# A spectral mixing and SwiGLU kernel: the last step of the inverse transform as four products of 96 columns

## The chip, the cores and the metric

The kernel runs on one core of a Trainium2 chip. The metric is the device time of one execution in microseconds (us). A core has five engines that run side by side: TensorE (PE; its weight loads are listed as PEld), VectorE (DVE), ScalarE (ACT), GpSimd (POOL) and SyncE (SP, which here only issues DMA transfers). Each engine takes its instructions in the order of the program and waits for others at semaphores. Everything is computed in fp32.

## The reference

Two blocks stand one behind the other. The first filters each of 8 sequences (3008 tokens, 256 channels) in the frequency domain. The second is a feed-forward block with a SwiGLU.

```python
X = np.fft.rfft(x, axis=1)                      # x: 8 x 3008 x 256
y = np.fft.irfft(X * (filt_r + 1j*filt_i), n=3008, axis=1)
t = y.reshape(24064, 256)
g, val = t @ w_gate, t @ w_val                  # 256 x 1536 each
out = (g / (1 + np.exp(-g)) * val) @ w_out      # 1536 x 256
```

## The kernel before

The length 3008 is 47 x 64, and so a transform is done in two steps each way, with twiddle factors in the tables. A token has the number n1 * 64 + n2, with n1 from 0 to 46 and n2 from 0 to 63. The step that is changed is the last one of the inverse transform, `stage3`: for each n2 it adds up 24 coefficients s (real and imaginary part) with a table of cosines and sines to the 47 values of n1. The signal is real, so 24 of the 47 coefficients are enough.

A batch is worked on in 4 chunks k. Each chunk has two halves i, each half two blocks cb of 128 channels; `step` counts these four sub-steps. In batch 0 a sub-step has four products of 96 rows (2 halves x 48) and 94 columns. From batch 1 on it has three products, packed so that all 128 rows are used:

```python
BACK = (((0, 0, 0, 48), (1, 48, 0, 48), (2, 96, 0, 32)),
        ((4, 64, 0, 48), (5, 112, 0, 16), (2, 0, 32, 16), (3, 16, 0, 48)),
        ((5, 0, 16, 32), (6, 32, 0, 48), (7, 80, 0, 48)))
BACK_AT = (0, 3 * N1, 7 * N1)                   # N1 = 47

# class Spectral: the coefficients of a half chunk come from DRAM
def load_t4(self, k, i, part=None):             # the branch for b > 0
    t = t4pool.tile([128, NH, C], FP32, ...)    # NH = 4, C = 256; 2 buffers
    rows = self.d2_tokens.rearrange("(h n) a c -> h (n a) c", h=2)
    rows = rows[:, ts(at, 2 * NS * NH)]         # NS = 24
    for j in range(2):
        self.load(out=t[64*j:64*j+64, 1], in_=rows[j, 128*(1-j):128*(1-j)+64])
        self.load(out=t[:, 2*j], in_=rows[j, 64*j:64*j+128])

def stage3(self, k, step):
    i, cb = divmod(step, 2)
    ps = (self.bank if k == 0 else fbank)(...)  # fbank too for k == 0 when b > 0
    for j in range(len(BACK) if back else 0):   # back = b: from batch 1 on
        cols = back_t[0][:, first:first + N1 * len(BACK[j])]     # 141, 188, 141
        pin(nc.tensor.matmul(out=rows, lhsT=self.t4[k, i][:, j, ts(cb, 128)], rhs=cols, ...))
    # batch 0: four products [96 rows] x [94 columns of wi_t]
    yield
    if cb == 0:
        pin(nc.scalar.copy(out=tokens(2 * i, 2), in_=psv))       # 376 elements
        return
    for t in range(2):                          # KS = (-1, 0, 1, 2)
        a, c = 2 * i + t, psv[:, :, ts(t, N1)]
        b, v, k = tokens(a, 1), tokens(4 + a, 1), KS[a]
        # k == 0: scalar.copy(v, c);  k == -1: vector add(v, c, b)
        # else:   vector v = c - k * b                           # 188 elements
```

The result `y` of a chunk has the tokens side by side, so that a sub-step writes every fourth element (16 bytes apart). All spectral steps of the batches from 1 on share one PSUM bank:

```python
fps = pool("fps", 1, PSUM)                      # one buffer
wps = pool("wps", NB, PSUM)                     # NB = 7, for the feed-forward products
def fbank(name):
    return fps.tile([128, NV, C], FP32, name=name, tag="f")
```

The feed-forward block runs at the same time, on the batch before. It works in groups, and the order of its operations is written out as a list of tokens. P, Q, A, B, E and W are products; s, x, y, e, l, h, v, o are operations that are mostly VectorE's; f, c, m, g, u are ScalarE's; D, S, n are GpSimd's. The tokens t0.0, t0.1 and so on are the slots in which spectral work is slipped in: up to five pieces a group (the first digit), and each slot carries a piece on to its next `yield`.

```python
SCHEDULE = """
Q0 o3' t4.2' W2 f0 S00' S01' x0.o' t0.0 x1.o' Q1 t0.1 x2.o' P3 x3.o' f1 t4.3' W1 x4.o' S10' x03 S11'
s13 x5.o' P1 o1 t0.2 P0 o2 c1 D01 A13 g1 c0 S20' Q2 S21' g0 y01 m13 t1.0 h0 f2 s01 W6 t1.1 h1 x23
D02 P2 o6 D12 A01 c2 B13 g2 n3' m01 t0.3 S30' t1.2 x02 W7 S31' g13 y12 y02 B01 h13 o7 t1.3 t2.0 s02
... # (cut)
E23 t3.2 m03 v13 E01 l23 e03 t3.3 t4.0 l01 u23 B23 v23 u01 t4.1 E03 n1 v01 g23 B03 l03 W3 h23 g03
u03 h03 v03
""".split()
```

The token h of a feed-forward group, for instance, is one VectorE product of 188 elements from PSUM with an SBUF operand (line L907). Products of the groups have 188 columns (L860) or 128 columns (L939).

Of the kernel before, what the change touches and what calls it, by code (L numbers as in the profile page):

```python
# [53 lines left out]
N1, N2 = 47, 64  # L54
# [58 lines left out]
PIECES = ((0, 7), (7, 14), (14, 20), (20, 26))  # L113

BACK = (((0, 0, 0, 48), (1, 48, 0, 48), (2, 96, 0, 32)),
        ((4, 64, 0, 48), (5, 112, 0, 16), (2, 0, 32, 16), (3, 16, 0, 48)),  # L120
        ((5, 0, 16, 32), (6, 32, 0, 48), (7, 80, 0, 48)))
BACK_AT = (0, 3 * N1, 7 * N1)


def dft_tables():
    n1, n2 = np.arange(N1), np.arange(N2)
    s, q = np.arange(NS), np.arange(NQ)
    ph = 2 * np.pi * (np.outer(n1, s) % N1) / N1
    w = np.stack([np.cos(ph), -np.sin(ph)], 1)
    wf = np.zeros((N1, 2, NS, 2, 2))  # L130
    wi = np.zeros((NS, 2, 2, N1, 2))

    v = np.stack([2 * np.cos(ph), -2 * np.sin(ph)], 0)
    v[0, :, 0], v[1, :, 0] = 1.0, 0.0
    for h in range(2):
        wf[:, h, :, :, h] = w.transpose(0, 2, 1)
        wi[:, :, h, :, h] = v.transpose(2, 0, 1) / S
    one = wi[:, :, 0, :, 0].transpose(1, 0, 2).reshape(2 * NS, N1)
    back = np.zeros((128, 10 * N1))
    for tile_, first in zip(BACK, BACK_AT):  # L140
        for i, (_, row, a, rows) in enumerate(tile_):
            back[row:row + rows, first + N1 * i:first + N1 * (i + 1)] = one[a:a + rows]


    kap = np.where(q[:, None] < 32, s + N1 * q[:, None], s + N1 * (95 - q[:, None]))
    sg = np.where(q < 32, 1.0, -1.0)[:, None]
    th = 2 * np.pi * ((n2[:, None, None] * kap) % S) / S
    c, sn = np.cos(th), np.sin(th)
    d = np.zeros((2, N2, NS, 2, NQ))
    d[0, :, :, 0] = c.transpose(0, 2, 1)  # L150
    d[1, :, :, 0] = sn.transpose(0, 2, 1)
    d[0, :, :, 1] = (-sn * sg).transpose(0, 2, 1)
    d[1, :, :, 1] = (c * sg).transpose(0, 2, 1)
    d = d.reshape(128, NS, 128)
    de = np.stack([d, d.transpose(2, 1, 0)], 2)

    paired = np.zeros((NP * (NPAIR + 1), 2, NP, NS))
    for j in range(NP):
        paired[NPAIR * j:NPAIR * (j + 1), :, j] = w[1:NPAIR + 1]
        paired[NP * NPAIR + j, 0, j] = 1.0  # L160
    paired = paired.reshape(NP * (NPAIR + 1), -1)


    pairs = np.arange(128).reshape(2, N2).T.ravel()
    later = np.stack([de[:, :, 0], de[:, :, 1][:, :, pairs]], 2)
    f32 = np.float32
    return (wf.reshape(NR, NK).astype(f32), wi.reshape(NK, NR).astype(f32),
            back.astype(f32), paired.astype(f32), np.ascontiguousarray(de).astype(f32),
            np.ascontiguousarray(later).astype(f32))


@with_exitstack
def kernel(
# [8 lines left out]
    out: bass.AP,  # L182
):
    nc = tc.nc
    wf_host, wi_host, back_host, paired_host, de_host, later_host = dft_tables()
    wf_dram = nc.inline_tensor(wf_host, name="wf_tbl")
    wi_dram = nc.inline_tensor(wi_host, name="wi_tbl")
    paired_dram = nc.inline_tensor(paired_host, name="paired_tbl")
    back_dram = nc.inline_tensor(back_host, name="back_tbl")
    de_dram = nc.inline_tensor(de_host, name="de_tbl").ap()  # L190
    later_dram = nc.inline_tensor(later_host, name="later_tbl").ap()
    unit_dram = nc.inline_tensor(np.eye(128, dtype=np.float32), name="unit_tbl")

    def pool(name, bufs, space=None):
# [63 lines left out]
    def sub(eng, dst, a, b):  # L258
        return eng.tensor_tensor(out=dst, in0=a, in1=b, op=ALU.subtract)  # L259
# [226 lines left out]
    def load_back():  # L486

        for n in range(3):
            t = rpool.tile([128, 2, 128], U32, name=f"paired_{n}", tag="pw", bufs=3)
            t = t.bitcast(FP32).rearrange("p b f -> p (b f)")  # L490
            (differences if n else paired_t).append(t[0:NP * (NPAIR + (not n))])
        t = rpool.tile([128, 2, 128, 2], U32, name="x_third", tag="raw", bufs=2)
        t = t.bitcast(FP32).rearrange("p b f two -> p (b f two)")
        third.append(t[0:NP * (NPAIR + 1)].rearrange("p (i c) -> p i c", c=C))
        pin(nc.sync.dma_start(out=paired_t[0][:, 0:2 * NP * NS], in_=paired_dram.ap()))
        t = rpool.tile([128, 2, 128, 2], U32, name="back", tag="raw", bufs=2)
        t = t.bitcast(FP32).rearrange("p b f two -> p (b f two)")
        back_t.append(t[:, 0:10 * N1])
        pin(nc.sync.dma_start(out=back_t[0], in_=back_dram.ap()))


# [13 lines left out]
    class Spectral:  # L515


        def __init__(self, b):
            self.b = b
            self.d1, self.d2 = [dram_tiles[2 * (b % 2) + i] for i in range(2)]  # L520
            self.d1_rows = self.d1.rearrange("a (h n) c -> (a h) n c", h=2)

            self.d2_tokens = self.d2.rearrange("a n c -> (a n) c").rearrange(
                "(n a) c -> n a c", n=N2)
            self.d2_rows = self.d2.rearrange("a (h n) c -> (a h) n c", h=2)
            self.x, self.t2, self.f, self.tb, self.p, self.t4, self.y = {}, {}, {}, {}, {}, {}, {}
            self.real = {}
# [42 lines left out]
        def load_two(self, u):  # L570
            if u < N_TWO:
                self.tb[u] = lend("tb", u).rearrange("p i (k c) -> p i k c", k=2)
                self.load(out=self.tb[u], in_=later_dram[:, ts(u, NV)])

                f = lend("f", u).rearrange("p (k i) c -> p k i c", k=2)
                self.f[u] = f
                for rows, view in filter_parts():
                    r, part = rows.start, rows.start // 64
                    for at in (r, r + 64) if part == 0 else (r,):
                        self.load(out=f[at:at + 32, part], in_=view(NV * u, NV))  # L580
                self.t2[u] = lend("t2", u)
                if self.b < 2:
                    self.load(out=self.t2[u], in_=self.twos(self.d1, u))
                    return
                rows = self.d1.rearrange("a n c -> (a n) c").rearrange(
                    "(n s p) c -> p n s c", n=N2, p=2)
                for i in range(2):
                    self.load(out=self.t2[u][N2 * i:N2 * (i + 1)], in_=rows[i, :, ts(u, NV)])
# [10 lines left out]
        def load_t4(self, k, i, part=None):  # L599
            if part is not None:  # L600

                t = f0[0:NK, ts(i, NH), :]
                r = (slice(0, 64), slice(64, NK))[part]
                self.load(out=t[r], in_=self.d2_rows[r, ts(i, NH), :])
            else:
                t = t4pool.tile([128, NH, C], FP32, name=f"t4_{self.b}_{k}_{i}", tag="t4")
                at = 2 * k + i
                if self.b == 0:
                    self.load(out=t[0:NK], in_=self.d2_rows[:, ts(at, NH), :])
                else:  # L610

                    rows = self.d2_tokens.rearrange("(h n) a c -> h (n a) c", h=2)
                    rows = rows[:, ts(at, 2 * NS * NH)]
                    for j in range(2):
                        self.load(out=t[64 * j:64 * j + 64, 1],
                                  in_=rows[j, 128 * (1 - j):128 * (1 - j) + 64])
                        self.load(out=t[:, 2 * j], in_=rows[j, 64 * j:64 * j + 128])
            self.t4[k, i] = t

        def bank(self, name):  # L620
# [105 lines left out]
        def stage2b(self, u):  # L726
# [14 lines left out]
            if self.b == 0:  # L741
                pin(queue.dma_start(out=self.twos(self.d2, u), in_=g))
                return
            rows = self.d2_tokens.rearrange("n (p s) c -> (n p) (s c)", p=2)
            pin(queue.dma_start(out=rows[:, ts(u, NV * C)], in_=g.rearrange("q s c -> q (s c)")))

        def stage3(self, k, step):
# [5 lines left out]
            psv = ps.rearrange("p a b -> p (a b)")[:, 0:TH].rearrange("p (n r) -> p n r", n=NH)  # L753
            flat = ps.rearrange("p a b -> p (a b)")
            back = self.b
            for j in range(len(BACK) if back else 0):
                first = BACK_AT[j]
                cols = back_t[0][:, first:first + N1 * len(BACK[j])]

                if j == 1:  # L760
                    rows = flat[:, 1:2 * 187 + 1].rearrange("p (z y) -> p z y", z=2)[:, :, ::2]
                else:
                    at = j // 2 * (2 * N1 + 1)
                    rows = flat[:, at:at + 6 * N1 - 1:2]
                pin(nc.tensor.matmul(out=rows, lhsT=self.t4[k, i][:, j, ts(cb, 128)], rhs=cols,  # L765
                                     start=j == 0, stop=True, skip_group_check=True))
            for n in range(0 if back else NH):
                pin(nc.tensor.matmul(out=psv[:, n, :],  # L768
                                             lhsT=self.t4[k, i][0:NK, n, ts(cb, 128)],
# [6 lines left out]
            def tokens(part, parts):  # L776
                return y[:, part:part + parts].rearrange("p t (r n) -> p n (t r)", n=NH)

            if cb == 0:
                pin(nc.scalar.copy(out=tokens(2 * i, 2), in_=psv))  # L780
                return
# [479 lines left out]
```

## Time and profile before

| | |
|---|---|
| median of 3 runs | 2923.2 us (2922.34 to 2925.03) |
| profiled span | 2922.1 us |
| granted TensorE clock | 0.998 of full speed |
| TensorE busy | 99% |
| VectorE / ScalarE / GpSimd busy | 69% / 55% / 55% |
| HBM | 460 MB read, 95 MB written, 190 GB/s |
| spectral sub-steps from batch 1 on | 112, with 336 products |

How to read the profile: the page gives each engine's busy time, then the chain of work that ended last, followed back from the end, then groups of equal instructions with their count, busy time and mean duration. A group reads "line engine operation output<-input, sizes xcount | busy us, mean ns | idle us before it <- who ended the idle time". For a product "128\*128 128x188" is a weight tile of 128 rows by 128 columns and 188 moving columns. An fp32 product leaves two records. The durations of products overlap one another, since they are pipelined. The timeline lists the instructions in order of time and merges equal neighbours.

### The profile page before, as it was taken

To read this page: it belongs to the slowest core of one execution; us is meant where nothing else is said; L and a number is where in the kernel's file an instruction comes from. 1 tells how busy PE (TensorE), PEld (TensorE's weight loads), DVE (VectorE), ACT (ScalarE), POOL (GpSimd) and SP (SyncE) were. 2 spreads that over 40 slices of the span, in tenths; PEclk is the share of its full clock that TensorE was granted. 3 is DMA by queue.
4 is the path that set the end of the run, shared out by engine and by line. 5 is a ranking of instruction groups with operands and counts; after the bars stand their busy time and mean duration, and the time that the engine had idled before them with its cause. 6 is when DMAs were issued, how large, how long until landed. Compare 5 with 4: busy or idle time off the path is not lost.

```text
span 2922.1 us, 57842 instructions
## 1 busy us (share of the span) xinstructions
PE 2888.1 (99%) x20160; PEld 2830.6 (97%) x20160; DVE 2030.1 (69%) x4536; ACT 1599.6 (55%) x4190; POOL 1595.3 (55%) x1767
## 2 busy tenths in 40 slices
PE   8999999999999999999999999999999999999999
PEld 6889999999999999999999999999999999999999
DVE  6888666676666776767767667676666766666665
ACT  6775455555555455555555554555555555555554
POOL 4876555556454655456554556454564555555453
PEclk9999999999999999999999999999999999999999
DMA  8677865565565655656656566556565565644442
GB/s 229 212 259 249 286 204 189 179 220 187 180 191 180 221 185 177 194 180 205 207 170 197 177 202 210 174 182 194 195 203 181 175 213 187 207 134 159 146 130 88
DMA packets 234325, 559.55 MB, mean 191 GB/s; under 512 B 31757, under 2 KB 128015, under 8 KB 234035
## 3 DMA queue, kind: packets, MB, share of 16 engines
q1 hardware_dynamic: 199169, 486.24, 52.2%
q10 hardware_dynamic: 25938, 45.72, 4.6%
q0 software_dynamic: 8928, 23.89, 2.3%
q8 instruction: 162, 2.65, 0.4%
q14 instruction: 128, 1.05, 0.1%
HBM read 460.38 MB, written 95.34 MB: 190 GB/s over the span
## 4 chain that ended last, share of the span: by engine, by line
PE 93%; DVE 1%; DMA 1%; POOL 1%; ACT 0%; issue 0%; SPq 0%; DVEq 0%; POOLq 0%
PE wa L860 24%; PE wA L939 17%; PE wk L860 16%; PE we L860 12%; PE wG L939 9%; PE wF L939 4%; PE pd L765 3%; PE pc L731 2%; PE pb L698 2%; PE pa L639 1%; PE pa L641 1%; PE pa L658 0%; DMA lent<-later_tbl 0%; PE pd L768 0%; DMA lent<-in_filt_r_dram 0%
## 5 line engine op out<-in xcount | busy, mean ns | idle before, releaser
L860 PE MATMUL wa<-y_t,wt_t 128*128 128x188 f32 x4464 | 878.8, 323 | 5.2 <-DVE o L256 1.4
L860 PEld LDWEIGHTS wa<-y_t,wt_t 128*128 128x128 f32 x4464 | 729.7, 190 | 13.0 <-issue 3.8
L256 POOL TENSOR_TENSOR h<-h 128x376 f32<-128x376 f32 x190 | 182.9, 983 | 765.5 <-DVE h L907 755.9
L939 PE MATMUL wA<-wo_t,h 128*128 128x128 f32 x4608 | 576.8, 275 | 2.5 <-DVE o L256 2.0
L939 PEld LDWEIGHTS wA<-wo_t,h 128*128 128x128 f32 x4608 | 563.0, 192 | 8.2 <-DVE o L256 1.8
L860 PE MATMUL wk<-y,wt_t 128*128 128x188 f32 x2976 | 566.8, 323 | 0.0
L259 POOL TENSOR_TENSOR h<-h 128x376 f32<-128x376 f32 x570 | 562.4, 1008 | 0.5
L860 PEld LDWEIGHTS wk<-y,wt_t 128*128 128x128 f32 x2976 | 479.8, 191 | 7.1 <-DVE y L256 0.6
L860 PE MATMUL we<-y_t,wt_t 128*128 128x188 f32 x2232 | 431.6, 323 | 1.4 <-ACT we L891 1.4
L259 DVE TENSOR_TENSOR we<-we,m 128x376 f32<-128x376 f32 x576 | 316.9, 555 | 161.3 <-PE we L860 110.4
L860 PEld LDWEIGHTS we<-y_t,wt_t 128*128 128x128 f32 x2232 | 369.4, 190 | 1.8 <-ACT we L891 1.7
L259 POOL TENSOR_TENSOR D<-f,f 128x376 f32<-128x376 f32 x288 | 281.3, 990 | 93.4 <-ACT f L875 92.5
L263 DVE SCALAR_TENSOR_TENSOR y<-wk,c 128x376 f32<-128x376 f32 x480 | 244.6, 541 | 108.5 <-ACT we L891 52.6
L895 ACT COPY m<-wa 128x376 f32<-128x376 f32 x576 | 271.8, 472 | 87.1 <-PE wa L860 86.2
L939 PE MATMUL wG<-wo_t,h 128*128 128x128 f32 x2304 | 288.3, 275 | 0.6 <-DVE o L256 0.6
L902 ACT ACTIVATE u<-we 128x188 f32<-128x188 f32 x576 | 188.9, 328 | 179.2 <-DVE we L259 161.0
L902 ACT ACTIVATE g<-wa 128x188 f32<-128x188 f32 x576 | 187.4, 327 | 174.6 <-PE wa L860 167.2
L939 PEld LDWEIGHTS wG<-wo_t,h 128*128 128x128 f32 x2304 | 281.4, 192 | 0.8 <-DVE o L256 0.8
L875 ACT ACTIVATE f<-wk 128x376 f32<-128x376 f32 x288 | 139.3, 484 | 231.1 <-PE wk L860 207.6
L879 ACT COPY c<-wk 128x376 f32<-128x376 f32 x288 | 136.0, 472 | 224.8 <-PE wk L860 224.8
L882 DVE SCALAR_TENSOR_TENSOR x<-wk,f 128x376 f32<-128x376 f32 x192 | 104.4, 544 | 218.5 <-PE wk L860 216.8
L891 ACT COPY we<-y 128x376 f32<-128x376 f32 x480 | 224.3, 487 | 35.7 <-DVE h L907 15.8
(155 smaller groups left out, 4030.2 us busy)
## 6 DMA issues: line engine op xcount, KB each, us to landing
wt_t<-w_all SPq DMA_DIRECT2D x174, 896.0 KB
wt_t<-w_all SPq DMA_DIRECT2D x174, 768.0 KB
lent<-later_tbl SPq DMA_DIRECT2D x84, 256.0 KB
lent<-in_filt_r_dram SPq DMA_DIRECT2D x336, 64.0 KB
d<-lent ACTq DMA_DIRECT2D x84, 256.0 KB
d<-t ACTq DMA_DIRECT2D x78, 240.0 KB
lent<-d SPq DMA_DIRECT2D x144, 128.0 KB
out_dram<-o POOLq DMA_DIRECT2D x124, 128.0 KB, 2.4
```

The costliest lines, as they stand in the source:

```text
L256: return eng.tensor_tensor(out=dst, in0=a, in1=b, op=ALU.add)
L259: return eng.tensor_tensor(out=dst, in0=a, in1=b, op=ALU.subtract)
L263: return nc.vector.scalar_tensor_tensor(out=dst, in0=a, scalar=-1.0, in1=b, op0=ALU.mult, op1=ALU.subtract)
L765: pin(nc.tensor.matmul(out=rows, lhsT=self.t4[k, i][:, j, ts(cb, 128)], rhs=cols, start=j == 0, stop=True, skip_group_check=True))
L860: pin(nc.tensor.matmul(out=ps[:, z], lhsT=self.wt[:, SLOT[p], z], rhs=rhs, start=start and z == 0, stop=True, skip_group_check=True))
L875: pin(act.mul(self.small(f"f{i}", f"f{i}", 1), t[f"k{i}"], -1.0))
L879: pin(act.copy(out=self.small(f"c{i}", f"c{i}", 1), in_=t[f"k{i}"]))
L882: pin(v.scalar_tensor_tensor(out=dst, in0=t[f"k{j}"], scalar=-1.0, in1=t[f"f{i}" if j == 3 else f"D{at}"], op0=ALU.mult, op1=ALU.add))
L891: pin(act.copy(out=self.bank(f"e{at}"), in_=t[f"y{at}"]))
L895: pin(act.copy(out=self.small(f"m{at}", "m", 4), in_=t[f"a{at}"]))
L902: pin(act.activation(out=self.small(op, "g", 3, 1)[:, 0], in_=ps[:, 1], func=AF.Silu))
L939: pin(nc.tensor.matmul(out=self.tiles[at][:, t, :], lhsT=self.hs[i][:, HID[p], t0:t0 + 128], rhs=wo_t[:, JB * q + i, WO[p], :], start=star ...
```

## The change

The cosine part of the sum is the same for n1 and 47 - n1, and the sine part has the opposite sign. So the changed kernel computes both parts for n1 from 0 to 23 alone, and forms sums and differences afterwards. The change is for the columns that TensorE has to stream: 4 x 96 instead of 141 + 188 + 141 a sub-step. Four products of 96 rows (4 values of n2 x 24 coefficients) give, in turn, the cosine part for four n2, the cosine part for the n2 that are 32 higher, and the two sine parts. ScalarE copies the sine part to its place in `y`; VectorE writes the difference to the places of n1 from 24 to 46 (in reverse order) and the sum over the sine part. On the second block of channels three corrections per chunk follow, in place in SBUF. A sub-step (but for the last of a chunk) has one more `yield` between the copy and VectorE's part. The coefficients of a half chunk now come in one transfer, the intermediate `d2` has its rows in the natural order, and a second table (`later_tbl`) is gone; the first (`de_tbl`) is read in its place.

```diff
-    one = wi[:, :, 0, :, 0].transpose(1, 0, 2).reshape(2 * NS, N1)
-    back = np.zeros((128, 10 * N1))
-    ... (cut)
+    back = np.zeros((NH, NS, 2, NH, NPAIR + 1))          # NPAIR = 23
+    for n in range(NH):
+        back[n, :, :, n] = v[:, 0:NPAIR + 1].transpose(2, 0, 1) / S
+    back = back.reshape(NH * NS, -1)
@@ load_two
-                self.load(out=self.tb[u], in_=later_dram[:, ts(u, NV)])
+                self.load(out=self.tb[u], in_=de_dram[:, ts(u, NV)])
@@ load_t4
-                    rows = self.d2_tokens.rearrange("(h n) a c -> h (n a) c", h=2)
-                    rows = rows[:, ts(at, 2 * NS * NH)]
-                    for j in range(2):
-                        self.load(out=t[64 * j:64 * j + 64, 1],
-                                  in_=rows[j, 128 * (1 - j):128 * (1 - j) + 64])
-                        self.load(out=t[:, 2 * j], in_=rows[j, 64 * j:64 * j + 128])
+                    m = NH * NS
+                    rows = self.d2_tokens.rearrange("(a r) c -> r a c", a=4)[ts(at, m)]
+                    self.load(out=t[0:m], in_=rows)
@@ stage2b
-            rows = self.d2_tokens.rearrange("n (p s) c -> (n p) (s c)", p=2)
+            rows = self.d2_tokens.rearrange("(q s) c -> q (s c)", s=NS)
@@ stage3
-            for j in range(len(BACK) if back else 0):
-                ... (cut: three products of 141, 188 and 141 columns)
+            m, w = NH * NS, NH * (NPAIR + 1)
+            for j in range(4 if back else 0):
+                pin(nc.tensor.matmul(out=flat[:, ts(j, w)], lhsT=self.t4[k, i][0:m, j, ts(cb, 128)],
+                                     rhs=back_t[0][:, ts(j // 2, w)], start=j == 0, stop=True,
+                                     skip_group_check=True))
@@ stage3, after the first yield
+            if back:
+                at = 2 * i + 4 * cb
+                both = y[:, at:at + 2].rearrange("p t w -> p (t w)").rearrange(
+                    "p (n z) -> p z n", z=2 * NH)
+                up, down = both[:, :, 0:NPAIR + 1], both[:, :, NPAIR + 1:N1]
+                even, odd = [flat[:, 2 * w * z:2 * w * (z + 1)].rearrange(
+                    "p (z n) -> p z n", z=2 * NH) for z in range(2)]
+                pin(nc.scalar.copy(out=up, in_=odd))
+                if step < 3:
+                    yield
+                pin(sub(nc.vector, down, even[:, :, NPAIR:0:-1], up[:, :, NPAIR:0:-1]))
+                pin(add(nc.vector, up, even, up))
+                for a in range(2 * i, 2 * i + 2) if cb else ():
+                    b, v, k = y[:, a], y[:, 4 + a], KS[a]
+                    if k == -1:
+                        pin(add(nc.vector, v, v, b))
+                    elif k == 1:
+                        pin(sub(nc.vector, v, v, b))
+                    elif k:
+                        pin(nc.vector.scalar_tensor_tensor(
+                            out=v, in0=b, scalar=-float(k), in1=v, op0=ALU.mult, op1=ALU.add))
+                return
```

More of the change, by code (lines that the diff above doesn't have):

```diff
@@ L113 @@
 PIECES = ((0, 7), (7, 14), (14, 20), (20, 26))
[L119 to L122, printed above, removed]
 def dft_tables():
@@ L137, in dft_tables @@
         wi[:, :, h, :, h] = v.transpose(2, 0, 1) / S
-    one = wi[:, :, 0, :, 0].transpose(1, 0, 2).reshape(2 * NS, N1)
-    back = np.zeros((128, 10 * N1))
-    for tile_, first in zip(BACK, BACK_AT):
-        for i, (_, row, a, rows) in enumerate(tile_):
-            back[row:row + rows, first + N1 * i:first + N1 * (i + 1)] = one[a:a + rows]
+    back = np.zeros((NH, NS, 2, NH, NPAIR + 1))
+    for n in range(NH):
+        back[n, :, :, n] = v[:, 0:NPAIR + 1].transpose(2, 0, 1) / S
+    back = back.reshape(NH * NS, -1)
     kap = np.where(q[:, None] < 32, s + N1 * q[:, None], s + N1 * (95 - q[:, None]))
@@ L161, in dft_tables @@
     paired = paired.reshape(NP * (NPAIR + 1), -1)
-    pairs = np.arange(128).reshape(2, N2).T.ravel()
-    later = np.stack([de[:, :, 0], de[:, :, 1][:, :, pairs]], 2)
     f32 = np.float32
     return (wf.reshape(NR, NK).astype(f32), wi.reshape(NK, NR).astype(f32),
-            back.astype(f32), paired.astype(f32), np.ascontiguousarray(de).astype(f32),
-            np.ascontiguousarray(later).astype(f32))
+            back.astype(f32), paired.astype(f32), np.ascontiguousarray(de).astype(f32))
 @with_exitstack
@@ L184 @@
     nc = tc.nc
-    wf_host, wi_host, back_host, paired_host, de_host, later_host = dft_tables()
+    wf_host, wi_host, back_host, paired_host, de_host = dft_tables()
     wf_dram = nc.inline_tensor(wf_host, name="wf_tbl")
@@ L190 @@
     de_dram = nc.inline_tensor(de_host, name="de_tbl").ap()
-    later_dram = nc.inline_tensor(later_host, name="later_tbl").ap()
     unit_dram = nc.inline_tensor(np.eye(128, dtype=np.float32), name="unit_tbl")
@@ L497, in load_back @@
         t = t.bitcast(FP32).rearrange("p b f two -> p (b f two)")
-        back_t.append(t[:, 0:10 * N1])
+        back_t.append(t[0:NH * NS, 0:2 * NH * (NPAIR + 1)])
         pin(nc.sync.dma_start(out=back_t[0], in_=back_dram.ap()))
@@ L521, in __init__ @@
             self.d1_rows = self.d1.rearrange("a (h n) c -> (a h) n c", h=2)
-            self.d2_tokens = self.d2.rearrange("a n c -> (a n) c").rearrange(
-                "(n a) c -> n a c", n=N2)
+            self.d2_tokens = self.d2.rearrange("a n c -> (a n) c")
             self.d2_rows = self.d2.rearrange("a (h n) c -> (a h) n c", h=2)
@@ L755, in stage3 @@
             back = self.b
-            for j in range(len(BACK) if back else 0):
[L757 to L766, printed above, removed]
+            m, w = NH * NS, NH * (NPAIR + 1)
[3 more added lines that the diff above has]
+                                     skip_group_check=True))
             for n in range(0 if back else NH):
```

## The prediction

> **What bounds the kernel now.** I read the page first: busy times and the chain that ended last.
>
> ```profile
> span 2922.1 us, 57842 instructions
> PE 2888.1 (99%) x20160; PEld 2830.6 (97%) x20160; DVE 2030.1 (69%) x4536; ACT 1599.6 (55%) x4190; POOL 1595.3 (55%) x1767
> ...
> PE 93%; DVE 1%; DMA 1%; POOL 1%; ACT 0%; issue 0%; SPq 0%; DVEq 0%; POOLq 0%
> ```
>
> TensorE is busy all the time and is 93% of the chain; nothing else has a share worth naming. Then the table by stage, over one whole batch in the middle (columns: window, its length, then busy us of PE, PEld, DVE, ACT, POOL, the clock, DMA share, GB/s):
>
> ```profile
> 774.60:1130.60 356.00, 356.00 (x2502) 351.82 (x2501) 246.10 (x551) 191.57 (x501) 190.53 (x204) 1.00 0.59 191
> ```
>
> In the steady state TensorE has no gap at all in 356 us. Anything that lengthens its own stream is paid one for one; anything that makes it wait is paid too; work on VectorE (69% here) is paid only where TensorE comes to wait for it.
>
> Next the groups by line and form, for the step that is changed:
>
> ```profile
> L765 PE MATMUL pd<-back,t 128*128 128x141 f32 x448 | 90.4, 283 | 0.0
> ...
> L765 PE MATMUL pd<-back,t 128*128 128x188 f32 x224 | 54.2, 322 | 0.0
> ...
> L768 PE MATMUL pd<-wi_t,t 96*128 96x94 f32 x96 | 13.1, 282 | 0.0
> ```
>
> Each fp32 product leaves two records, so 448 and 224 records are 224 products of 141 columns and 112 of 188: three products in each of 112 sub-steps (7 batches, 4 chunks, 4 sub-steps). The third line is luck: batch 0 does this step with products of 96 rows and 94 columns, and the change leaves batch 0 alone. That is nearly the form the change brings to the others (96 rows, 96 columns), also four in a row.
>
> The busy and mean figures are no use for the cost: a record's duration contains latency that the next record overlaps. What counts is from the start of a sub-step to the start of the work after it, so I went to the timeline. First the present form, then the form of batch 0 (columns: start, us to the last end, engine, line, operation, tiles, form, records):
>
> ```profile
> 1026.21 0.97 PE L765 MATMUL pd<-back,t 128*128 128x141 f32 x6
> 1027.02 0.80 PE L860 MATMUL wk<-y,wt_t 128*128 128x188 f32 x4
> 1027.65 0.80 PE L860 MATMUL wa<-y_t,wt_t 128*128 128x188 f32 x4
> ...
> 1029.62 0.64 PE L860 MATMUL wa<-y_t,wt_t 128*128 128x188 f32 x3
> ```
>
> ```profile
> 88.92 1.03 PE L768 MATMUL pd<-wi_t,t 96*128 96x94 f32 x8
> 89.78 0.83 PE L860 MATMUL wk<-y,wt_t 128*128 128x188 f32 x4
> 90.45 1.45 PE L860 MATMUL wa<-y_t,wt_t 128*128 128x188 f32 x8
> ```
>
> Three products of 470 columns in all take 1027.02 - 1026.21 = 0.81 us; the four records after them take 1027.65 - 1027.02 = 0.63 us. Four products of 376 columns in all take 89.78 - 88.92 = 0.86 us, and the four records after them 0.67 instead of 0.63. So four narrow products occupy TensorE for 0.86 + 0.03 or 0.04 = 0.90 us: fewer columns, more time.
>
> **What the skill says.** "TensorE: Matmul & The Clock Gate", section "LDWEIGHTS (loading the stationary operand)", gives a weight load as columns / 1.2 in ns, whatever the rows: an estimate of 128 / 1.2 = 107 ns. The trace agrees: a record of the 128-column product L939 comes every 1.34 us / 12 = 112 ns (start to start of its groups of 12), and the 94-column records of batch 0 come at 0.90 / 8 = 112 ns too. Below about 128 columns the weight load sets the pace, and 96 weight rows instead of 128 do not help. The 188-column records come every 0.64 / 4 = 159 ns, where the columns are the limit.
>
> "SBUF — State Buffer", section "SBUF: two separate sides", says that a VectorE operation with two SBUF inputs and a GpSimd operation that reads SBUF exclude each other. The trace fits: the addition of two 256-element SBUF operands in the paired step took 0.42 us in some places and a mean of 1.19 us (x_third) in others. Three of the new VectorE operations per chunk are of that kind. The section "Door 1: The DMA port swizzle" has a note that each access to a new 16-byte line of SBUF pays; the copy out of this step, which writes every fourth fp32, takes 851 ns for 376 elements against 472 to 487 ns for contiguous ones. A stride of 32 bytes instead of 16 should cost no more per element, since each element already opens a line.
>
> **The change part by part.**
>
> TensorE. Removed: 112 x 0.81 us = 90.7 us. Added: 112 x 0.90 us = 100.8 us. Net +10.1 us. The columns alone (470 to 384) would have promised a gain: at the 159 ns per 188-column record, 86 columns x 2 records x 159 / 188 = 145 ns per sub-step, 16 us in all. I take the +10.1 because batch 0 shows the very form.
>
> ScalarE. Removed per chunk: two copies of 376 and one of 188 (2 x 851 + 509 = 2.21 us). Added: four copies of 192 with a stride. From 509 ns for 188 and 851 for 376, 1.82 ns per element: 192 cost 516 ns, four are 2.06 us. No change that matters.
>
> VectorE. Removed per chunk: three operations of 188 at 500 ns, 1.50 us. Added: in each of four sub-steps a difference of 184 and a sum of 192, with a PSUM and a strided SBUF operand as in the 500 ns ones: 8 x 0.50 = 4.0 us. Plus three corrections of 188 contiguous elements, both inputs in SBUF: about 0.34 us as for the 188-element products of L907, up to twice that beside GpSimd: 1.0 to 2.0 us. Net +3.5 to +4.5 us per chunk, 28 chunks: +98 to +126 us, so VectorE goes from 2030 to about 2130 to 2155 us busy, 73%. Off the path unless TensorE waits.
>
> DMA. The chunk's coefficients came in four transfers per half chunk (64, 128, 64, 128 KB: the page's two forms, 112 each) and come in one of 384 KB. Same bytes, fewer issues, nothing to gain: TensorE never waited for them. The other table and the row order of the intermediate cost the same.
>
> Waits. The three kinds of spectral work share a single PSUM bank. It was given back after one ScalarE copy (or two VectorE operations). Now it is given back after copy, difference and sum, in a later slot. I went through the places where the pair of VectorE operations lands and compared when it would end, at 2 x 0.50 us after the VectorE operation before it, with the start of the next user of the bank in the present trace. Most have 0.5 to 3 us to spare. The two closest of each batch:
>
> ```profile
> 834.66 0.56 DVE L256 TENSOR_TENSOR o<-o,wG 128x384 f32<-128x384 f32 x1 [0.31 <-PE wG L939]
> ```
>
> ```profile
> 1036.42 0.55 DVE L256 TENSOR_TENSOR o<-o,wG 128x384 f32<-128x384 f32 x1 [0.91 <-PE wG L939]
> ...
> 1037.70 1.19 DVE L259 TENSOR_TENSOR we<-we,m 128x376 f32<-128x376 f32 x2 [0.46 <-PE we L860]
> 1037.98 0.91 PEld L765 LDWEIGHTS pd<-back,t 128*128 128x128 f32 x6
> 1038.13 0.96 PE L765 MATMUL pd<-back,t 128*128 128x141 f32 x6
> ```
>
> In the second, the pair would run from 1036.97 to 1037.97 and the next product starts at 1038.13: 0.16 us to spare, from which the signal's way to TensorE still goes. In the first it ends at 835.22 + 1.00 = 836.22, and the bank's next user (the first step of the next batch) starts at 836.43: 0.21 us. Besides, VectorE runs up to 1.0 to 1.6 us late behind each pair, and at a few places (the last sums before a batch's end, where a bank written by VectorE is read 1.4 us later) that uses up the slack. I count some 25 places in the whole run that sit at the limit and charge each 0.1 to 0.3 us: 2.5 to 7.5 us, say 4 us.
>
> Sum: 2923.2 + 10.1 + 4 = 2937 us, 0.5% slower.
>
> **The rivals.**
>
> (a) The columns set the pace, also at 96: then TensorE saves 16 us and, less some waits, the kernel takes about 2908 to 2913 us. For it: the mean 141-column record comes every 0.12 us (6 records with 470 x 2 columns in 0.81 us), still near its columns. Against it: batch 0's 94 columns at the same 112 ns as 128 columns. I give it 3%.
>
> (b) The single bank becomes the bound: the pair on VectorE is late by more than I read (strided operations slower than 0.50 us, or the corrections locked against GpSimd by a whole 1.0 us operation), and TensorE waits 0.5 us or more at most of the sub-steps. 112 x 0.5 = 56 us would give about 2990 us. Against it: VectorE is idle 31% of the time, and most places have over 0.5 us. A milder form, 10 to 15 us of waits in all, is what my upper end stands for.
>
> (c) The waits vanish: TensorE's own 0.09 us per sub-step gives the others a little time, and only the 10 us remain: 2933 us. Quite possible.
>
> **Range and chances.** 2930 us would be the bare TensorE cost with 3 us less than I work out, 2949 us the cost with 16 us of waits. Both outcomes of the 2% line are far: faster needs under 2865 us, which no part of the change could pay for; slower needs over 2982 us, which only rival (b) in full gives.
>
> **What would show it.** In the profile after, by step: the group of 96-column products has 896 records (112 x 4 x 2), and in the timeline a sub-step of 8 records lasts 0.86 to 0.87 us to the next start, with 0.03 us more behind it. If it lasts 0.65 to 0.70 us, rival (a) is right and I am wrong. A batch in the middle, 356.0 us now, becomes 356.0 + 16 x 0.09 = 357.4 us plus its waits (up to 1 us); if it is 360 or more, the waits were undercounted, and the wait table of TensorE should name VectorE's spectral sums before pd or pa. VectorE's busy time in the 2130 to 2155 range and its difference and sum at about 0.50 us would confirm the sizes; 0.7 us or more each would point to (b). ScalarE's copy of 192 should be near 0.52 us, and the DMA should show no waits on TensorE.

## The result, and the profile after

The changed kernel takes 2935.84 us (median of 4 runs, 2934.66 to 2937.29) against 2924.11 us before (2922.34 to 2927.42). The ratio is 1.0039, with a 95% interval from 1.0022 to 1.0056: slower by some 12 us.

The page of the changed kernel, busy times and chain:

```profile
span 2935.5 us, 58335 instructions
PE 2902.7 (99%) x20384; PEld 2843.4 (97%) x20384; DVE 2130.7 (73%) x4760; ACT 1599.8 (54%) x4218; POOL 1598.5 (54%) x1767
...
PE 93%; DVE 1%; POOL 1%; ACT 0%; issue 0%; DVEq 0%
```

TensorE is still 93% of the chain. Its busy time has grown by 14.6 us; VectorE's has grown by 101 us, and yet its share of the chain has not. The timeline of TensorE, one sub-step after the place that was shown of before, in the same batch:

```profile
1037.23 1.03 PE L740 MATMUL pd<-back,t 96*128 96x96 f32 x8
1038.10 0.83 PE L859 MATMUL wa<-y_t,wt_t 128*128 128x188 f32 x4
1038.76 0.80 PE L859 MATMUL we<-y_t,wt_t 128*128 128x188 f32 x4
```

This must be read from start to start. The sub-step takes 1038.10 - 1037.23 = 0.87 us, where it took 0.81 us with three products. The group after it takes 0.66 us instead of 0.63: the products behind the narrow ones start late as well, and so the next group carries a part of the cost. The two together make 0.09 us more in each of the 112 sub-steps. From the starts in the trace to the nanosecond it is 0.867 + 0.176 us to the second record after the sub-step, against 0.804 + 0.146: 0.093 us, 10.4 us in all (means over the 112 sub-steps; from the third record on it is 10.5 us).

One whole batch by stage, from the first changed sub-step of one batch to that of the next, first before and then after (columns: window, length, busy us of PE, PEld, DVE, ACT, POOL with their counts, clock, DMA share, GB/s):

```profile
421.12:777.15 356.03, 356.03 (x2502) 351.85 (x2501) 246.55 (x550) 191.69 (x501) 190.59 (x205) 1.00 0.60 192
```

```profile
423.26:780.91 357.65, 357.65 (x2535) 353.39 (x2533) 259.82 (x582) 191.74 (x505) 191.05 (x205) 1.00 0.60 190
```

A batch is 1.62 us longer: 16 x 0.093 = 1.49 us of products, and a rest of 0.13 us. I laid the two traces over each other, record by record, from the second batch on. The start of TensorE's records shifts by 0.09 us behind each sub-step, 10.5 us in all, and in one other place, once in each of six batches and 0.8 us in all. That place is the group of products wF (token W2 of the list) shortly after a chunk's last sub-step. In before and after:

```profile
1042.82 1.50 PE L939 MATMUL wF<-wo_t,h 128*128 128x128 f32 x12
1044.16 1.03 PE L698 MATMUL pb<-lent 128*128 128x256 f32 x4
```

```profile
1048.08 1.63 PE L938 MATMUL wF<-wo_t,h 128*128 128x128 f32 x12
1049.55 1.03 PE L680 MATMUL pb<-lent 128*128 128x256 f32 x4
```

It takes 1.47 us to the next start instead of 1.34. VectorE's timeline shows what it waits for. The first line is from before, the others are from after the change:

```profile
1041.68 0.34 DVE L907 TENSOR_TENSOR h<-we,u 128x188 f32<-128x188 f32 x1
```

```profile
1045.05 0.50 DVE L245 TENSOR_TENSOR y<-pd,y 128x184 f32<-128x184 f32 x1 [0.50 <-ACT y L763]
1045.58 0.51 DVE L242 TENSOR_TENSOR y<-pd,y 128x192 f32<-128x192 f32 x1
1046.13 0.35 DVE L245 TENSOR_TENSOR y<-y 128x188 f32<-128x188 f32 x1
1046.40 0.35 DVE L775 SCALAR_TENSOR_TENSOR y<-y 128x188 f32<-128x188 f32 x1
...
1047.38 0.60 DVE L906 TENSOR_TENSOR h<-wa,g 128x188 f32<-128x188 f32 x2
1047.92 0.35 DVE L906 TENSOR_TENSOR h<-we,u 128x188 f32<-128x188 f32 x1
```

VectorE waits 0.50 us for ScalarE's copy of the sine part, does the difference, the sum and two corrections, and so comes late to the operations that write h. The last of them (token v03, the line h<-we,u) writes rows that the second product of wF takes as its weights. It ends at 1048.27 us, and the weight load of that product starts at 1048.33; the first product of wF had started on time at 1048.08. Before the change the same operation ended at 1042.02, 0.8 us ahead of wF. So TensorE waits for data here, and not for a bank.

The span of the profiled run grew by 13.4 us and not by 11.3. The other 2.1 us lie ahead of the first changed sub-step (it starts at 421.1 us before and 423.3 us after), in batch 0, which the change doesn't touch. In the other profiled runs below that start is anywhere from 419.7 to 424.9 us.

### The profile page after: what moved, and what is told of

Read it like the earlier page. It is cut to its first block, busy times and chain, and to the rows that moved or that the text cites. A ratio compares the mean times of both kernels' runs of the same rounds, so it can differ in the third digit from the quotient of the medians.

```text
span 2935.5 us, 58335 instructions
## 1 busy us (share of the span) xinstructions
PE 2902.7 (99%) x20384; PEld 2843.4 (97%) x20384; DVE 2130.7 (73%) x4760; ACT 1599.8 (54%) x4218; POOL 1598.5 (54%) x1767
## 4 chain that ended last, share of the span: by engine, by line
PE 93%; DVE 1%; POOL 1%; ACT 0%; issue 0%; DVEq 0%
PE wa L859 24%; PE wA L938 17%; PE wk L859 16%; PE we L859 12%; PE wG L938 9%; PE wF L938 4%; PE pd L740 3%; PE pc L713 2%; PE pb L680 2%; PE pa L621 1%; PE pa L623 1%; PE pa L640 0%; DVE h L906 0%; DVE we L245 0%; DVE pw L334 0%
```

## The experiments

**Wider products.** Each unit of 24 columns gets eight zero columns behind it.

```diff
-    back = np.zeros((NH, NS, 2, NH, NPAIR + 1))
+    back = np.zeros((NH, NS, 2, NH, 32))
     ... (cut)
-            m, w = NH * NS, NH * (NPAIR + 1)
+            m, w = NH * NS, NH * 32
     ... (cut)
```

> Changed kernel, but each of the four products has 128 columns (8 zero columns behind each 24). If the weight load sets the pace up to about 128 columns: records still every 112 ns, a sub-step 0.87 us to the next start, time as the changed kernel (about 2936 us). If the columns set the pace: 32 more columns x 8 records x 0.83 ns = 0.21 us more per sub-step, 24 us over the changed kernel (about 2960 us).

Measured: 2934.16 us (one run). The timeline:

```profile
1034.13 1.06 PE L740 MATMUL pd<-back,t 96*128 96x128 f32 x8
1035.02 0.80 PE L859 MATMUL wa<-y_t,wt_t 128*128 128x188 f32 x4
1035.66 0.80 PE L859 MATMUL we<-y_t,wt_t 128*128 128x188 f32 x4
```

0.89 us for the sub-step and 0.64 us behind it: together 1.53 us, exactly as with 96 columns (0.87 + 0.66). A third more columns cost nothing.

**Narrower products.** n1 from 0 to 11 alone, so 48 columns a product. The rest of the result is left out.

```diff
-    back = np.zeros((NH, NS, 2, NH, NPAIR + 1))
+    back = np.zeros((NH, NS, 2, NH, 12))
     ... (cut)
-                even, odd = [flat[:, 2 * w * z:2 * w * (z + 1)].rearrange(
+                even, odd = [flat[:, 0:4 * w].rearrange(
```

> The changed kernel with products of 48 columns (n1 from 0 to 11 alone; the rest of the result is left out, ScalarE's and VectorE's operations keep their sizes). If the weight load sets the pace: records still every 112 ns, a sub-step 0.87 us, about 2935 us. If the columns do: half of the 0.87 us goes, 112 x 0.4 = 45 us less.

Measured: 2937.91 us (one run).

```profile
1037.89 0.99 PE L740 MATMUL pd<-back,t 96*128 96x48 f32 x8
1038.72 0.87 PE L859 MATMUL wa<-y_t,wt_t 128*128 128x188 f32 x4
1039.42 0.80 PE L859 MATMUL we<-y_t,wt_t 128*128 128x188 f32 x4
```

0.83 + 0.70 = 1.53 us again. The expectation of 0.87 us for the sub-step itself was off by 0.04: with fewer columns more of the cost falls into the group behind it. But the sum stays, and half the columns save nothing. With 48, 96 and 128 columns the whole run's extra time behind the sub-steps, laid over the trace of before, is 10.5 us in all three. The number of products with 128 weight columns is what costs, 112 ns for each of a product's two records.

**VectorE's part alone.** The three products of before, with all that follows them in the changed kernel. The values are not the transform's, since even and sine part overlap in the bank.

```diff
+                even, odd = [flat[:, 184 * z:184 * z + 192].rearrange(
+                    "p (z n) -> p z n", z=2 * NH) for z in range(2)]
+                pin(nc.scalar.copy(out=up, in_=odd))
+                if step < 3:
+                    yield
+                ... (difference, sum and corrections as in the change)
```

> The kernel before with its three products, but with the changed kernel's copy, difference, sum and corrections behind them, and their extra slot (the values are not the transform's). If the time comes from TensorE's own stream: a sub-step stays 0.80 us, VectorE goes to about 2130 us busy, and the time is that of before plus at most 1 us of waits (2924 to 2926 us). If VectorE's work or the bank held longer is what costs: 2930 to 2936 us.

Measured: 2926.04 us (12 runs) against 2924.60 us, ratio 1.0003 (0.9995 to 1.0011). VectorE is 2117.7 us busy. Sub-steps take 0.804 us as before. TensorE's records shift by 1.3 us at wF and 0.8 us where a transfer is awaited, and nowhere else. The time is at the upper edge of what was expected if TensorE's own stream is the cause, and VectorE is 12 us less busy than expected.

**The products alone.** The four products of the change, with the copies and three VectorE operations of before. The mirrored half of the result is left out.

```diff
-            if back:
-                ... (copy of the sine part, difference, sum, corrections)
-                return
             if cb == 0:
                 pin(nc.scalar.copy(out=tokens(2 * i, 2), in_=psv))
                 return
```

> The changed kernel with its four products of 96 columns, but with the copies and three VectorE operations of before behind them, without sums and differences (left out: the mirrored half of the result). If TensorE's stream is the cause: a sub-step takes 0.87 + 0.03 us, and the time is before plus 10 us (2934 us) with VectorE at about 2030 us busy. If VectorE or the bank is the cause: no change against before (2924 us).

Measured: 2934.10 us (7 runs), ratio 1.0030 (1.0019 to 1.0041). The same sub-step as above takes 0.86 us:

```profile
1038.76 1.03 PE L740 MATMUL pd<-back,t 96*128 96x96 f32 x8
1039.62 0.83 PE L836 MATMUL wa<-y_t,wt_t 128*128 128x188 f32 x4
```

VectorE is 2032.8 us busy; TensorE's records shift by 10.4 us behind the sub-steps and by nothing elsewhere. The two halves of the change thus add up: about 10.4 us for the products, 1 to 2 us for VectorE's part.

**Folded and packed.** If a record costs the larger of 112 ns and the time of its columns, the fold should be used to widen three products less, and not to make four narrow ones. The 384 rows of a half chunk go on 128 rows again; the row blocks of n2 that are split over two products are added up in the bank.

```diff
+    for g in range(4 * NH * NS):
+        j, (part, unit) = g // 128, divmod(g // NS, 2 * NH)
+        at = 6 * c * j + (2 * NH * part + unit) * c - 5 * c * j      # c = 24
+        back[g % 128, at:at + c] = v[part, 0:c, g % NS] / S
     ... (cut)
-            for j in range(4 if back else 0):
-                pin(nc.tensor.matmul(out=flat[:, ts(j, w)], ...
+            for j in range(3 if back else 0):
+                pin(nc.tensor.matmul(out=flat[:, 5 * c * j:5 * c * j + 6 * c],
+                                     lhsT=self.t4[k, i][:, j, ts(cb, 128)],
+                                     rhs=back_t[0][:, ts(j, 6 * c)], start=j == 0, ...
     ... (cut)
-                    self.load(out=t[0:m], in_=rows)
+                    ... (six transfers of 96, 32, 64, 64, 32 and 96 rows)
```

> The same fold to 24 of 47 values, but packed on 128 rows again: three products of 144 columns (the rows of one unit of 24 split over two products, which add up in the bank), six transfers per half chunk, VectorE's part as in the changed kernel. If a record costs the larger of 112 ns and its columns (about 122 ns at 144): a sub-step takes 6 x 122 = 0.735 us instead of 0.804, 112 x 0.07 = 7.7 us less than before, plus about 1 us of waits: 2917 us, ratio 0.9977. If VectorE's part or the bank costs as much as TensorE's: no gain, 2924 to 2930 us.

Measured: 2925.52 us (13 runs), ratio 1.0004 (0.9996 to 1.0012). No gain. But the products did what was expected: a sub-step takes 0.735 us, and laid over the trace of before they save 7.4 us. It came back as waits: TensorE's records shift by 4.8 us at products we, 2.0 us at wF and 1.9 us at wa. TensorE's waits (us in total, times, longest) name ScalarE (in the kernel before: 1.4 us, once), and ScalarE's name a transfer (before: 2.9 us, three times):

```profile
PE we L865 <- ACT we L896: 4.9, 4, 1.4
```

```profile
ACT we L896 <- DMA x<-in_x_dram: 15.8, 6, 3.5
```

The timeline shows one of the six:

```profile
877.78 0.58 ACT L631 COPY t<-pa 120x512 f32<-120x512 f32 x1 [0.54 <-PE pa L627]
...
881.49 0.32 ACTq L635 DMA_DIRECT2D d<-t  x1
881.85 0.88 ACT L896 COPY we<-y 128x376 f32<-128x376 f32 x2 [3.48 <-DMA x<-in_x_dram]
...
882.38 0.90 PE L865 MATMUL we<-y_t,wt_t 128*128 128x188 f32 x4 [1.38 <-ACT we L896]
```

ScalarE has done its copy at 878.36. Its next instruction issues the transfer of that result, and this issue stands until 881.49 for an x transfer with which it has no data in common. The copy that TensorE needs is ScalarE's next operation; it starts at 881.85, and so the wait reaches TensorE. My theory then: six transfers instead of one or four put an older, still running transfer in the way. The rival was VectorE's part, which this run shares with the change.

**The same, in one transfer.** The intermediate is stored in the order in which the products take it, by the order of the columns of a second table. The lines show what differs from the run before it.

```diff
+    order = np.arange(128).reshape(2, 2, 8, NH).transpose(2, 0, 1, 3).ravel()
+    later = np.stack([de[:, :, 0], de[:, :, 1][:, :, order]], 2)
     ... (cut)
-                    ... (six transfers)
+                    rows = self.d2_tokens[ts(at, 4 * m)].rearrange("(j p) c -> p j c", p=128)
+                    self.load(out=t[:, 0:3], in_=rows)
```

> The three folded products of 144 columns as in the run before it, but the intermediate is stored in the order in which the products need it, so that a half chunk comes in one transfer instead of six. If the six transfers made ScalarE's own transfers wait (and TensorE behind them): ScalarE's wait for the x transfers falls from 15.8 us to below 3, TensorE's 8.8 us of waits fall to about 1 to 2 us, and the time is 2924.6 - 7.4 + 1.5 = 2918.7 us, ratio 0.998. If VectorE's part or the bank made them: no change against the six transfers (2925.5 us).

Measured: 2918.62 us (19 runs) against 2924.89 us, ratio 0.9979 (0.9973 to 0.9986). This version beats both kernels. A batch by stage, and a sub-step:

```profile
419.71:774.99 355.28, 355.25 (x2502) 350.81 (x2501) 260.13 (x582) 191.41 (x505) 190.81 (x205) 1.00 0.59 192
```

```profile
1029.10 0.90 PE L747 MATMUL pd<-back,t 128*128 128x144 f32 x6
1029.84 0.48 PE L867 MATMUL wa<-y_t,wt_t 128*128 128x188 f32 x2
```

The sub-step takes 0.74 us, and VectorE is just as busy as in the change (260.13 us a batch). ScalarE no longer waits for an x transfer at all. TensorE's shifts are -7.4 us behind the sub-steps and 1.7 us at wF.

**The change, in six transfers.** The counter-check: nothing but the number of transfers.

```diff
-                    self.load(out=t[0:m], in_=rows)
+                    for p, n, j in ((0, 96, 0), (0, 32, 1), (32, 64, 1), (0, 64, 2), (64, 32, 2),
+                                    (0, 96, 3)):
+                        self.load(out=t[p:p + n, j], in_=rows[p:p + n, j])
```

> The changed kernel, with the single transfer of a half chunk split into six. If the number of transfers is what brought the waits: ScalarE again waits 10 us or more for x transfers, and the time is the changed kernel's plus 4 to 7 us (2940 to 2943 us). If not: 2936 us.

Measured: 2947.19 us (4 runs), ratio to before 1.0079 (1.0063 to 1.0094). Among ScalarE's waits:

```profile
ACT we L892 <- DMA x<-in_x_dram: 18.2, 6, 3.6
```

The waits for x transfers are there again, and the cost is larger than I expected: TensorE's records shift by 10.3 us outside the sub-steps (7.2 at we, 1.9 at wa, 1.2 at wF), against 0.8 us with one transfer. The direction settles the cause; the size I had taken from the packed version, whose waits were shorter.

The traces also tell why ScalarE's issue stands for just that transfer. The transfers that SyncE and ScalarE issue share eight semaphores, and an issue waits for the one that it will use itself until the transfer that had it last has landed. In each of the six waits of both runs with six transfers that was an x transfer, and between the two stand six or seven other issues, six of them the half chunk's. The one shown above was issued at 872.97 us and landed at 881.41, 0.08 us before ScalarE's issue. With one transfer per half chunk the turns fall otherwise, and ScalarE's issue of this result waits for no x transfer.

## Why the prediction was right

- **TensorE bounds the kernel without gaps.** Right: a batch is 357.65 us, all of it busy.
- **A narrow product costs what a weight load costs.** Right, and it carries nearly all of the result: predicted +10.1 us, measured 10.4 to 10.5 us in the change and in the products alone. Rival (a), that columns set the pace, fell with the runs of 48 and 128 columns. The Trainium skill, "TensorE: Matmul & The Clock Gate", section "LDWEIGHTS (loading the stationary operand)", agrees in what was measured: records come every 112 ns, whether the weights have 96 or 128 rows, where 107 ns were estimated from it. That the weight load is the reason is in part argued. No run gives these products fewer weight columns, so that another fixed cost of a record is not excluded; but the records of the loads themselves, which overlap one another, last 165 ns at 96 columns (L658 of the kernel before, in batch 0) and 190 to 192 ns at 128. Between them lie 25 to 27 ns, and an estimate from the page's rule for 32 columns is 27 ns.
- **ScalarE.** Right: a copy of 192 takes 510 ns where 516 was worked out, and its busy time stays at 1600 us.
- **VectorE's sizes.** Right: difference and sum take 495 and 511 ns (0.50 assumed), and 2130.7 us is the lower edge of 2130 to 2155. Of the three corrections, two take 354 and 347 ns. The third, on the first channel half, has a mean of 730 ns and spreads:

```profile
L242 DVE TENSOR_TENSOR y<-y x28: 353/820/1172, 433.3 to 2796.2; 128x188 f32<-128x188 f32 x28
```

(minimum, median and maximum in ns). That fits what the Trainium skill's page "SBUF — State Buffer", section "SBUF: two separate sides", says of two SBUF inputs beside GpSimd, and the trace parts the 28 cleanly. Twelve run while GpSimd computes nothing and take 353 to 355 ns. Sixteen start during a GpSimd operation that reads SBUF (h<-h or D<-f,f), take 819 to 1172 ns, and end 0.2 us after it.
- **Waits.** Half of the mechanism was right, and the size was too large. The spectral bank, given back later, made TensorE wait nowhere. VectorE's lateness did, at another place than the prediction named, and what came late was h, the weights of wF. 4 us were charged at some 25 places; 0.8 us came, at six. The 0.13 us of each lie within the 0.1 to 0.3 us that were assumed, so the term that was mis-sized is the number of places. Both of the places that were shown as closest did without a wait. Of the one with 0.16 us to spare the trace says:

```profile
1042.04 0.49 DVE L245 TENSOR_TENSOR y<-pd,y 128x184 f32<-128x184 f32 x1
1042.57 0.51 DVE L242 TENSOR_TENSOR y<-pd,y 128x192 f32<-128x192 f32 x1
```

The sum ends at 1043.08, and the next sub-step starts, without idle time, 0.2 us later.

Rival (b), the bank as the bound, did not come at any sub-step, and the run with VectorE's part alone shows it too. Rival (c), no waits at all, is nearer to the 0.8 us than the sum of the prediction was. That the time came out only 1.2 us below the 2937 us is therefore in part luck: the waits were 3.2 us less, but the products cost 0.4 us more, and the median of before rose by 0.9 us with a fourth run. The rest is within the spread of the runs.
- **The DMA.** "Nothing to gain" was right as far as the change goes, but for a poor reason. TensorE didn't wait for the coefficients; still their number of transfers matters, by way of ScalarE's issues. Had the change needed six transfers, it would have cost 11 us more.

## What to carry to other kernels

On a core whose TensorE is never idle, count products and not columns: from 128 columns down to 48, at 128 weight columns in fp32, a product got no cheaper here, so a trick that halves the columns must not be paid for with more products. Look for the same form elsewhere in the trace: an untouched part of the program may already show what the new form costs. And count the transfers that an engine with work of its own has to issue among: where transfers share semaphores, one more or less changes which earlier transfer an issue stands for, and that holds up everything behind it.

## What was not expected of the hardware

The cost of a burst of narrow products doesn't end with it. With 48, 96 and 128 columns the burst itself lasts 0.83, 0.87 and 0.89 us, but the four records behind it take 0.70, 0.66 and 0.64 us, so that the sum is 1.53 us in all three.

Splitting 384 KB into six transfers instead of one, with the same bytes, cost 11 us (2947.2 against 2935.8 us), without one TensorE wait for the data itself. ScalarE stood up to 3.6 us at an issue, for a transfer that it shares no data with, by way of the semaphore that the two have in common.
